# Two stacked layers of segment-recurrent attention and gated MLP: Q and K of four segments' own tokens computed ahead, kept in DRAM and read back

## The chip, the cores and the metric

The kernel runs on one core of a Trainium2 chip. The metric is the device time of one execution in microseconds (us): the median of the runs. Five engines work side by side, each on its own instructions in order: PE (TensorE; matmuls, and as PEld its weight loads), DVE (VectorE), ACT (ScalarE), POOL (GpSimd) and SP (SyncE), which issues most DMA transfers. ACT and POOL issue some as well.

## What is computed

```python
def _A_ref(x, mem0, Wq, Wk, Wv, Wo, seg_len):      # 2048 tokens of width 576, 64 segments of 32
    mem = mem0                                     # 8 memory tokens
    for s in range(n_seg):
        xs = x[:, s * seg_len:(s + 1) * seg_len, :]
        h = concatenate([mem, xs])                 # 40 rows
        q, k, v = h @ Wq, h @ Wk, h @ Wv           # 32 heads of 128
        p = softmax(where(mask, q @ k.T * scale, -1e9))
        o = einsum("hte,hed->td", p @ v, Wo)
        mem = o[:, :M]                             # the next segment's memory
        outs.append(o[:, M:])
def _B_ref(x, w1, w3, w2):                         # hidden width 4608
    return (silu(x @ w1) * (x @ w3)) @ w2
x = x + _A_ref(_layernorm(x), ...); x = x + _B_ref(_layernorm(x), ...)
x = x + _A_ref(_layernorm(x), ...); x = x + _B_ref(_layernorm(x), ...)
```

The memory makes the segments a recurrence: segment s+1 can start only when segment s has its output. The own 32 tokens of a segment in the first layer, though, depend on x alone.

## The kernel before

The work is a sequence of 72 steps. Step t handles segment t of the first layer and, from step 8 on, segment t-8 of the second (LAG = 8). Steps 0 to 7 and 64 to 71 have one layer and 40 columns; steps 8 to 63 have both, 80 columns side by side. After four segments a block of 128 tokens goes through the MLP, spread over later steps.

A step's attention works in four groups (g) of eight heads. For each of eight units (u) of four heads, qk does 32 matmuls (Q and K, four heads, four chunks of 128 of the width) and qk_tail 8 half-row matmuls for the last 64 of the width. qk_ev copies the result from PSUM to QKT, one of four buffers, in two pieces where there are two layers. Then come scores (bank<-QKT), the softmax on DVE and ACT (tiles SME, STAT, PB), the transposition of P (in one-layer steps on PE; in the others a DMA transpose issued by SP, PTS<-PB), P times V, the output projection (wo, wo_tail), and the copy of the new memory into HT. V is projected by vm, vx and vg.

All parts of the work are nodes with dependencies, buffers and modelled costs. The order of PE's nodes is written out by hand as a string of letters: FIRST for steps 0 to 15, then FOUR eleven times for four steps each, then LAST. plan places the nodes of the other engines (and of SP's DMA queue) around it by modelled times, choosing DVE or ACT for copies. Every engine then runs its list in order. The table WARM names places where em.warm issues filler matmuls (line 663), which compute nothing that is used. The weights Wq, Wk, Wv and Wo, 18.9 MB, are loaded in that order at the start by SP, with their tails and the first block of x partly by ACT; then the MLP's weights stream through two buffers each (W13, W2C).

x_in brings a block of 128 rows of x into XN; ln_stats, ln_pow, ln_norm and ln_tr normalise and transpose it, and ht_write puts it into HT, from which qk reads. The MLP's input is XTB.

Of the kernel before, what the change touches and what calls it, by code (L numbers as in the profile page):

```python
# [7 lines left out]
BF = mybir.dt.bfloat16  # L8
# [5 lines left out]
P = 128  # L14
# [16 lines left out]
WARM = {("QKt", 5): 22, ("TR", 2): 8, ("VMt", 1): 8, ("PV", 1): 5, ("TR", 3): 2, ("QK", 9): 2, ("PV", 5): 2, ("WO", 5): 3, ("TR", 7): 2, ("QK", 17): 2, ("SC", 12): 1,  # L31
        ("PV", 9): 2, ("WO", 9): 2, ("PV", 11): 1}
# [11 lines left out]
         "xr": 3, "xn": 2, "w13": 2, "w2": 2, "htt": 3}  # L44
# [14 lines left out]
class Node:  # L59
# [11 lines left out]
    def after(self, *more):  # L71
        for d in more:
# [7 lines left out]
         "WO": "O", "WOt": "o", "VX": "X", "VXt": "x", "VM": "V", "VMt": "v", "FF": "F", "FFt": "f", "VG": "G", "VGt": "g", "W2": "W", "W2b": "w"}  # L80
# [126 lines left out]
def ewh(*ns):  # L207
# [5 lines left out]
    "amQqqQQqqQSqQQqTSqSQqQTSVvxXPPTTOoPPOOooOoQqqqQQSQqQSvQqqqVTSPOQqQTTSPPXoOTOPoxOooQQqqqqQSQvVqSQQqQqqQSSTTPPOoOT"  # L213
    "TPoPOOooaVvqqQQQqqSQQSqqqQQQSTxqPTSOPXOTTooPPOOooQqqqpQQSQqVSnQvfqFqQQSfFqqQTFTSPfPTOOWoofPTFPOOooFfqqQQQSWQFqqf"
    "qQFTSqfVvqqQQQWTSSPFPFffXxWTOPoOTOPFOoooffFQqqqQWQQSFfqqVvfFQWSqQQSTFqqffQFTSPaWPOTOPFooffTFPOOooWqqQQQSqqQVSvqf"
    "FQTQWQqqqTPSQObSPoXXTTxxPOPOOoooQpQQqqqqQnSvqSFfVFfqQQQSFfqQqWSPFFPffOoOPWOFPooOofFQqqfqQWSQQQQqqqfFSFSGqfgqQQWP"
    "GSgfgFGPFOofgGPOWPOOoooFfqqQQQSfqqFWQFvSqfVQQqWSFqfqQQfPPSFOOFooPWaffOPFOooWQqqqqQQbSQQQqqSGSqgqQQPgGSOoPGggGPOO"
    "PooOoQqppQQQqqqVnnSSvfFQFfqqQQQqqfSFSwPWPOOFooffFPWPOwOooFqqffQFQWwSFfqqQQQWQqqSwSfgfGFPFQQqqGSggGPGOOPoogfFPOOo"
    "owQWQffqqFFQwQqqSWSvVqqqQQQFffSqFQPwWPSFffOOFPawooOPWOooFfqqQQWSQqqqqQQQSwbqqSQQGgSggGPGPOGogPOPOOooo"
# [23 lines left out]
def make_nodes(em, nseg, pools, o=Opt, dma_bw=230e3, load_bw=400e3):  # L243
# [125 lines left out]
    def step(t):  # L369
# [18 lines left out]
        for g in range(NG):  # L388
            qs, qe = [], []
            for u in (2 * g, 2 * g + 1):  # L390
                q = Slot("qkt", users=1)
                b = banks()
                pq = t + o.qk + o.ustep * u
                m_ = node("PE", 32 * mm80 + (0.02 if nl == 1 else 0.0), em.qk(t, u, b), deps=hx + hm[:1] + ([ld_h[u // 4]] if t == 0 else []),
                          prio=pq, mode="full", acq=[q] + b, name="QK")
                n = node("PE", 4 * mm80 + (0.014 if nl == 1 else 0.008), em.qk_tail(t, u, b), deps=hx + hm + ([ld_h[u // 4]] if t == 0 else []), prio=pq + o.qkt, mode="row",
                         acq=[q] + b, name="QKt")
                rd += [m_, n]
                me[f"QK{u}"], me[f"QKt{u}"] = m_, n
                for r in (0, 1):  # L400
                    qe.append(node("AD", ew(256, 64) if nl == 2 else ew(160), em.qk_ev(t, u, r, q, b[r]), deps=[m_, n], prio=t + o.ustep * u,
                                   rel=[b[r]], name="QKe"))
                qs.append(q)
# [73 lines left out]
    def job(j):  # L477
# [45 lines left out]
        for pp, ents, at in todo:  # L523
# [4 lines left out]
            for pr_ in (2 * pp, 2 * pp + 1):  # L528
# [8 lines left out]
                else:  # L537
# [3 lines left out]
                    ld = [node("DMA", kb(1152, 256) / dma_bw, em.load_w13(pr_, w13), prio=prio - 1, acq=[w13], lat=2.3, name="W13")]  # L541
                    lds.append(node("DMA", kb(256, 576) / dma_bw, em.load_w2(pr_, w2), prio=prio - 0.99, acq=[w2], lat=2.2, name="W2l"))
# [55 lines left out]

    x_in(0)
    ht_mem[0] = [node("DVE", 0.1, em.init_mem(0, 0), deps=[m0e], prio=-4, name="m0")]  # L600
# [27 lines left out]
class Emitter:  # L628
# [137 lines left out]
    def load_xn(self, g, xn):  # L766
        return lambda n: (self.dma if g else self.adma)(self.T.XN[:, xn.i, 0:D], self.a.x[g * P:(g + 1) * P, :])
# [70 lines left out]
    def ln_pow(self, xn):  # L838
        def f(n):
            L = self.T.LNS[:, xn.i]  # L840
            self.ch("POOL", self.nc.gpsimd.tensor_tensor(L[:, 15:16], L[:, 14:15], self.T.mhalf[:], op=ALU.pow))
        return f

    def ln_norm(self, src, xn):
        def f(n):
            L = self.T.LNS[:, xn.i]
            self.v("tensor_scalar", self.T.XN[:, xn.i, 0:D], self.src_ap(src), L[:, 12:13], L[:, 15:16],
# [124 lines left out]

    def head(self, g, j):

        return GH * g + j

    def qk(self, t, u, b):

        def f(n):
# [3 lines left out]
            for c in range(4 if first and t == 0 and u % 4 == 0 else 0):  # L983
                for _ in range(3):
                    self.mm(self.bk(b[1])[:], self.T.ident[:, 0:P], self.T.W[:, 4 + c, u * 512:(u + 1) * 512], True, True)
            for j in range(4):
                h0 = self.head(u // 2, 4 * (u % 2) + j) * E
                for kind in (0, 1):
                    for c in range(4):
                        self.mm(self.bk(b[kind])[:, j * SW:j * SW + q1 - q0], self.T.W[:, 4 * kind + c, h0:h0 + E], HTt[:, c, q0:q1],  # L990
# [3 lines left out]
    def qk_tail(self, t, u, b):  # L994
        def f(n):
            q0, q1 = self.qcols(t)
            HTt = self.ht(t)
            first = self.begin(b)
            for j in range(4):
                h0 = self.head(u // 2, 4 * (u % 2) + j) * E  # L1000
                for kind in (0, 1):
                    rr = slice(kind * R64, (kind + 1) * R64)
                    self.mm(self.bk(b[kind])[:, j * SW:j * SW + q1 - q0], self.T.W[rr, 8, h0:h0 + E], HTt[rr, 4, q0:q1],
# [313 lines left out]
def kernel(  # L1317
# [42 lines left out]
    T.mhalf = sp.tile([P, 1], F32, name="mhalf")  # L1360
# [6 lines left out]
    T.LNS = sp.tile([P, pools["xn"], 16], F32, name="LNS")  # L1367
    T.QKT = sp.tile([P, pools["qkt"], 2, 4, 2 * QW], BF, name="QKT")
# [11 lines left out]
    T.HTT = sp.tile([P, pools["htt"], 2, 2 * P], BF, name="HTT")  # L1380
    T.M0 = T.XTB[:].rearrange("p a b -> p (a b)")[:, 0:D]
# [3 lines left out]
    nc.gpsimd.memset(T.mhalf[:], -0.5)  # L1385
# [60 lines left out]
```

## Time and profile before

| | us |
|---|---|
| median of 3 runs (lowest to highest) | 2618.39 (2617.04 to 2626.04) |
| the profiled execution, its own time | 2624.02 |
| its span in the trace | 2622.2 |
| PE busy | 2567.1 |
| DVE busy | 2009.5 |
| ACT busy | 1266.8 |
| mean granted clock of PE | 0.999 |

The span is the time between the first and the last event of the trace. A busy PE counts filler matmuls as well as work, and the ends of matmuls are modelled, since they are pipelined: the spacing of many in a row says what one costs, not the duration of a single one. An idle time is put down to what ended last before the instruction could go; "issue" is a wait for nothing that the profile shows.

### The profile page before, as it was taken

The page shows a single profiled execution, that of the slowest core. Times are in us where ns is not written, and L with a number is a line of the kernel's source. Part 1 is how long each engine was busy: PE and PEld are TensorE (multiplying, and loading weights), DVE is VectorE, ACT ScalarE, POOL GpSimd, SP SyncE. Part 2 cuts the span into 40 slices and gives each one's busy share as a digit, 9 for nine tenths or more (in the row PEclk, how much of TensorE's full clock was granted, in tenths as well). Part 3 has the DMA queues.
Part 4 walks back from the last instruction along what each step waited for, and adds up shares of the span by engine and source line. Part 5 has one row for each costly group of instructions (what it writes and reads, how often), then busy time and mean ns, then how long its engine had stood idle before and what let it go on. Part 6 is the DMA issues. An engine that isn't in the chain of part 4 may idle for free.

```text
span 2622.2 us, 131462 instructions
## 1 busy us (share of the span) xinstructions
PE 2567.1 (98%) x58447; PEld 2205.6 (84%) x58498; DVE 2009.5 (77%) x5145; ACT 1266.8 (48%) x3743; POOL 196.1 (7%) x253
## 2 busy tenths in 40 slices
PE   6999999999999999999999999999999999999998
PEld 4788888888888888888888888888888888888887
DVE  4778777787787688777867877786787778777877
ACT  2655453544545354454535445453544545445553
POOL 1100000000001000000000000010000000010000
PEclk9999999999999999999999999999999999999999
DMA  9064746565464656555465655546465554554447
GB/s 326 4 181 126 193 103 154 126 152 136 126 139 115 148 128 153 135 126 141 115 148 128 155 133 127 144 109 151 128 156 132 126 143 112 128 146 129 123 131 258
DMA packets 680217, 369.58 MB, mean 141 GB/s; under 512 B 233592, under 2 KB 669824, under 8 KB 679008
## 3 DMA queue, kind: packets, MB, share of 16 engines
q1 hardware_dynamic: 675968, 353.23, 52.5%
q8 instruction: 457, 7.49, 1.2%
q0 software_dynamic: 3024, 6.93, 0.9%
q10 hardware_dynamic: 656, 1.02, 0.2%
q14 instruction: 112, 0.92, 0.1%
HBM read 304.95 MB, written 2.36 MB: 117 GB/s over the span
## 4 chain that ended last, share of the span: by engine, by line
PE 90%; DMA 4%; DVE 3%; SPq 1%; issue 1%; ACT 1%; ACTq 0%; DVEq 0%
PE bank L653 90%; DMA PTS<-PB 2%; DMA W<-in_B_w_dram 1%; SPq L672 1%; DVE STAT L669 1%; DVE PB L669 1%; DVE SME L669 1%; DMA WV<-in_A_Wv_dram 0%; DVE HTT L669 0%; DMA W<-in_A_Wk_dram 0%; ACT V L666 0%; DVE V L669 0%; PE bank L663 0%; DMA W2C<-in_B_w_dram 0%; ACT HT L666 0%
## 5 line engine op out<-in xcount | busy, mean ns | idle before, releaser
L653 PEld LDWEIGHTS <-W 128*128 128x128 bf16 (+2 forms) x32096 | 1252.3, 100 | 121.3 <-issue 66.1
L653 PE MATMUL bank<-HT,W 128*128 128x80 bf16 (+3 forms) x23040 | 792.9, 197 | 9.6 <-ACT HT L666 5.4
L653 PE MATMUL bank<-XTB,W 128*64 128x256 bf16 (+5 forms) x9056 | 662.5, 264 | 4.5 <-DMA W<-in_B_w_dram 4.2
L666 ACT ACTIVATE QKT<-bank 128x192 bf16<-128x192 f32 (+4 forms) x1674 | 382.2, 312 | 274.5 <-PE bank L653 268.7
L653 PE MATMUL bank<-OT,WO 128*128 128x80 bf16 (+3 forms) x11520 | 411.1, 198 | 1.3 <-issue 1.3
L653 PEld LDWEIGHTS <-WO 128*128 128x128 bf16 (+1 forms) x11520 | 380.4, 102 | 27.6 <-issue 13.4
L666 ACT ACTIVATE V<-bank 64x512 bf16<-64x512 f32 (+1 forms) x589 | 333.0, 585 | 136.7 <-PE bank L653 129.8
L653 PE MATMUL bank<-WV,HT 128*32 128x512 bf16 (+4 forms) x3430 | 355.9, 381 | 6.8 <-issue 4.3
L653 PE MATMUL bank<-W2C,HTT 128*64 128x288 bf16 (+1 forms) x3152 | 322.1, 287 | 0.7 <-DMA W2C<-in_B_w_dram 0.6
L666 ACT ACTIVATE HTT<-bank 128x512 bf16<-128x512 f32 (+1 forms) x324 | 173.1, 550 | 284.0 <-PE bank L653 283.1
L669 DVE SCALAR_TENSOR_TENSOR XR<-bank,XR 128x288 f32<-128x288 f32 x574 | 243.4, 448 | 59.0 <-PE bank L653 53.4
L669 DVE TENSOR_REDUCE STAT<-SME 104x8 f32<-104x320 f32 (+1 forms) x576 | 273.8, 475 | 12.2 <-ACT SME L666 5.0
L669 DVE TENSOR_TENSOR PB<-SME,STAT 40x128 bf16<-40x128 f32 (+4 forms) x912 | 275.1, 336 | 8.1 <-issue 0.2
L653 PEld LDWEIGHTS <-HT 128*32 128x32 bf16 (+4 forms) x3472 | 147.5, 98 | 140.3 <-issue 24.9
L1092 POOL MEMSET PB<- 128x1024 bf16 x142 | 134.8, 951 | 1742.7 <-DMA PTS<-PB 1219.4
L653 PEld LDWEIGHTS <-HTT 128*64 128x64 bf16 (+1 forms) x3232 | 231.4, 105 | 35.7 <-issue 5.6
L669 DVE SCALAR_TENSOR_TENSOR HTT<-HTT,bank 128x512 bf16<-128x512 bf16 (+1 forms) x324 | 200.9, 620 | 69.7 <-ACT HTT L666 65.8
L666 ACT ACTIVATE OT<-bank 128x320 bf16<-128x320 f32 (+1 forms) x389 | 145.1, 402 | 203.8 <-PE bank L653 196.6
L669 DVE TENSOR_TENSOR HTT<-HTT,bank 128x512 bf16<-128x512 bf16 (+1 forms) x324 | 203.5, 628 | 28.0 <-DVE HTT L669 0.9
L666 ACT ACTIVATE SME<-SME 104x320 f32<-104x320 f32 (+1 forms) x288 | 135.0, 469 | 180.9 <-DVE SME L669 179.0
L669 DVE CAST V<-bank 64x512 bf16<-64x512 f32 (+1 forms) x275 | 188.3, 685 | 40.8 <-PE bank L653 36.4
L669 DVE TENSOR_TENSOR SME<-bank,maskb 104x320 f32<-104x320 f32 (+1 forms) x288 | 138.9, 483 | 39.4 <-PE bank L653 36.1
(61 smaller groups left out, 1400.8 us busy)
## 6 DMA issues: line engine op xcount, KB each, us to landing
W<-in_B_w_dram SPq DMA_DIRECT2D x604, 256.0 KB, 3.5
W2C<-in_B_w_dram SPq DMA_DIRECT2D x302, 288.0 KB, 3.5
W<-in_B_w_dram SPq DMA_DIRECT2D x604, 32.0 KB, 3.5
W<-in_B_w_dram SPq DMA_DIRECT2D x8, 1024.0 KB, 13.0
W<-in_A_Wq_dram SPq DMA_DIRECT2D x9, 512.0 KB, 9.9
WO<-in_A_Wo_dram SPq DMA_DIRECT2D x4, 1152.0 KB, 16.8
XR<-in_A_x_dram POOLq DMA_DIRECT2D x16, 288.0 KB, 2.9
WV<-in_B_w_dram SPq DMA_DIRECT2D x4, 1152.0 KB, 12.3
```

Of the source, the lines that this page charges most:

```text
L653: self.ch("PE", self.nc.tensor.matmul(out, lhsT=lhsT, rhs=rhs, start=start, stop=stop, skip_group_check=True, **k))
L666: self.ch("ACT", self.nc.scalar.activation(*a, **k))
L669: self.ch("DVE", getattr(self.nc.vector, fn_)(*a, **k))
L672: self.ch("SP", self.nc.sync.dma_start(out=out, in_=in_))
L1092: return lambda n: self.ch("POOL", self.nc.gpsimd.memset(self.pbt(pb), 0.0))
```

## The change

A new function hold, called after the first block of x, loads two more blocks of x (rows 256 to 511, segments 8 to 15) on ACT's DMA queue, normalises and transposes them, and copies the even segments 8, 10, 12 and 14 into XTB. Eight units (KP with 32 matmuls, KPt with 8) multiply these 128 columns with Wq and Wk, two copies bring each unit's result from PSUM into a W2C buffer (KPe), and SP stores it to a DRAM tile SX (KPs). In steps 8, 10, 12 and 14 (PRE) the matmuls of qk and qk_tail take 48 columns where they took 80: the second layer's 40 and the first layer's 8 memory columns, read as two pieces of 24. A load by SP (KPl) brings the unit's 64 KB into QX, one buffer, and a copy (KPc) puts it into QKT; qk_ev copies three pieces. The MLP's weight loads come after the last store. The constant of ln_pow moves into the tile LNS. FIRST and WARM are written anew; FOUR and LAST are as they were.

```diff
-WARM = {("QKt", 5): 22, ("TR", 2): 8, ("VMt", 1): 8, ("PV", 1): 5, ("TR", 3): 2, ("QK", 9): 2, ("PV", 5): 2, ("WO", 5): 3, ("TR", 7): 2, ("QK", 17): 2, ("SC", 12): 1,
-        ("PV", 9): 2, ("WO", 9): 2, ("PV", 11): 1}
+WARM = {("QKt", 1): 30, ("Ktr", 2): 10, ("KPt", 1): 1, ("SC", 4): 1, ("VXt", 1): 6, ("PV", 1): 2, ("WO", 1): 1}
+PRE = (8, 10, 12, 14)
...
-    "amQqqQQqqQSqQQqTSqSQqQTSVvxXPPTTOoPPOOooOoQqqqQQSQqQSvQqqqVTSPOQqQTTSPPXoOTOPoxOooQQqqqqQSQvVqSQQqQqqQSSTTPPOoOT"
+    "amcqcqkQQKkqSqQQqKqSQQqkTQSQqTSxXVvKPTOPoTPOPOooOoQqqqQQSQqqqVvQqSQQQSTqXqxPSTKPOTOPooTOPokOoaQqqqQSVvqqqQQSQQqq"
...
+                if held:
+                    x = Slot("qx")
+                    ld = node("DMA", kb(P, 256) / load_bw, em.held_load(t, u, x), deps=[held_st[u]], prio=pq - 0.5, acq=[x], lat=2.2, name="KPl")
+                    qe.append(node("AD", (0.05 + 256 / 1200, 0.065 + 256 / 1920), em.held_copy(u, q, x), deps=[ld, m_], prio=pq, rel=[x], name="KPc"))
...
-                    ld = [node("DMA", kb(1152, 256) / dma_bw, em.load_w13(pr_, w13), prio=prio - 1, acq=[w13], lat=2.3, name="W13")]
+                    ld = [node("DMA", kb(1152, 256) / dma_bw, em.load_w13(pr_, w13), deps=held_st[-1:], prio=prio - 1, acq=[w13], lat=2.3, name="W13")]
...
+    def hold():
+        wr = []
+        for i in (0, 1):
+            xn = Slot("xn")
+            ld = node("ACT", 0.6, em.load_xn(PRE[2 * i] // 4, xn, True), prio=-70 + i, acq=[xn], name="ldxn", lat=9.0)
+            wr += ln_nodes("K", xn, xn, [ld], -3 + i, [(em.held_write(i), ewh(320), [m0t])])
+        mm = (P / 2.4 + 2.5) / 1000
+        for u in range(8):
+            b = banks()
+            prio = 0.5 + 0.1 * u
+            m_ = node("PE", 32 * mm, em.held_qk(u, b, False), deps=wr + [ld_h[u // 4]], prio=prio, mode="full", acq=b, name="KP")
+            n = node("PE", 4 * mm + 0.008, em.held_qk(u, b, True), deps=wr + [ld_h[u // 4]], prio=prio, mode="row", acq=b, name="KPt")
+            w = Slot("w2")
+            es = [node("AD", ew(512), em.held_ev(r, w, b[r]), deps=[m_, n], prio=prio, acq=[w], rel=[b[r]], name="KPe") for r in (0, 1)]
+            held_st.append(node("DMA", kb(P, 1024) / load_bw, em.held_store(u, w), deps=es, prio=prio, rel=[w], lat=2.2, name="KPs"))
+            last_up.extend([m_, n])
...
+    def held_cols(self, v):
+        return bass.AP(v.tensor, v.offset, [list(x) for x in v.ap][:-1] + [[QW + 16, 2], [1, 24]])
...
+            elif self.held(t):
+                self.cp(n, dst[:, :, 64:SW], src[:, :, 0:16])
+                self.cp(n, dst[:, :, 0:MEM], src[:, :, 16:24])
+                self.cp(n, dst[:, :, QW:64], src[:, :, 24:48])
```

In the letters c is a new transposition, K and k the new units' matmuls and tails.

On VectorE, the first instructions after the clearing of the banks. Before:

```order
L669 BN_STATS LNS<-XN 128x6 x2
L669 BN_AGGR LNS<-LNS 128x2
L669 TENSOR_SCALAR LNS<-LNS 128x1
L669 TENSOR_SCALAR XN<-XN,LNS 128x576
L669 COPY XN<-XN 128x64
```

And in the changed kernel:

```order
11 L696 BN_STATS LNS<-XN 128x6 x2
12 L696 BN_AGGR LNS<-LNS 128x2
13 L696 TENSOR_SCALAR LNS<-LNS 128x1
14 L696 BN_STATS LNS<-XN 128x6 x2
15 L696 BN_AGGR LNS<-LNS 128x2
16 L696 TENSOR_SCALAR LNS<-LNS 128x1
17 L696 TENSOR_SCALAR XN<-XN,LNS 128x576
18 L696 COPY XN<-XN 128x64
```

The statistics of the second block (rows 14 to 16) now stand ahead of the normalisation of the first (rows 17 and 18), which PE's first transposition reads.

On SP, the issues after the four loads of Wo. Before (W_84 is the tile W13, the MLP's up weights, W2C its down weights):

```order
8 L672 DMA WO<-in_A_Wo_dram 128x8x576 x4
9 L672 DMA W_84<-in_B_w_dram 128x4x256 x2
10 L672 DMA W_84<-in_B_w_dram 64x256 x2
11 L672 DMA W2C<-in_B_w_dram 128x2x576
12 L672 DMA W_84<-in_B_w_dram 128x4x256 x2
```

And now (SX is the DRAM tile, QX the buffer of the loads back):

```order
8 L699 DMA WO<-in_A_Wo_dram 128x8x576 x4
9 L699 DMA SX<-W2C 128x4x256 x2
10 L699 DMA QX<-SX 128x256
11 L699 DMA SX<-W2C 128x4x256
12 L699 DMA XN<-in_A_x_dram 128x576
13 L699 DMA SX<-W2C 128x4x256 x5
14 L699 DMA W_83<-in_B_w_dram 128x4x256 x2
```

The eight stores and the first load back stand where the first weights of the MLP stood; these follow the last store.

On SP in step 10, about the DMA transposes of P (PTS<-PB). Before:

```order
104 L1095 DMA_TRANSPOSE PTS<-PB 128x8x112 x2
105 L672 DMA W2C<-in_B_w_dram 128x2x576 x2
106 L672 DMA W_84<-in_B_w_dram 128x4x256 x2
107 L672 DMA W_84<-in_B_w_dram 64x256 x2
108 L1095 DMA_TRANSPOSE PTS<-PB 128x8x112
109 L672 DMA W_84<-in_B_w_dram 128x4x256 x2
```

And in the changed kernel:

```order
110 L699 DMA QX<-SX 128x256
111 L699 DMA W_83<-in_B_w_dram 128x4x256 x2
112 L699 DMA W_83<-in_B_w_dram 64x256 x2
113 L699 DMA QX<-SX 128x256
114 L699 DMA W2C<-in_B_w_dram 128x2x576 x2
115 L699 DMA QX<-SX 128x256
116 L699 DMA W_83<-in_B_w_dram 128x4x256 x2
117 L699 DMA W_83<-in_B_w_dram 64x256 x2
118 L1180 DMA_TRANSPOSE PTS<-PB 128x8x112
```

The loads back stand between the weight loads and the transposes, one by one.

More of the change, by code (lines that the diff above doesn't have):

```diff
@@ L764, in load_o, with load_xn @@
         return lambda n: self.dma(self.T.WO[:, g * GH:(g + 1) * GH, :], self.a.wo[g * GH:(g + 1) * GH].rearrange("h e d -> e h d"))
[L766 to L767 removed]
+    def load_xn(self, g, xn, early=False):
+        return lambda n: (self.dma if g and not early else self.adma)(self.T.XN[:, xn.i, 0:D], self.a.x[g * P:(g + 1) * P, :])
     def load_x(self, g, xr):
```

85 lines of the change are left out of this document (67 added, 18 removed).

## The prediction

> **What bounds the kernel now.** I read the page first: busy shares, the slices, the chain that ended last.
>
> ```profile
> PE 2567.1 (98%) x58447; PEld 2205.6 (84%) x58498; DVE 2009.5 (77%) x5145; ACT 1266.8 (48%) x3743; POOL 196.1 (7%) x253
> PE   6999999999999999999999999999999999999998
> DMA  9064746565464656555465655546465554554447
> PE 90%; DMA 4%; DVE 3%; SPq 1%; issue 1%; ACT 1%; ACTq 0%; DVEq 0%
> ```
>
> TensorE carries the time, except in the first slice, where it is 60% busy and the DMA engines are full. Whatever saves matmul time saves time, if nothing else then ends last. Next, the busy time in stretches; columns are the stretch, then its length, busy time of PE, PEld, DVE, ACT, POOL, the granted clock, DMA share, GB/s. The cuts at 59, 82, 103 and 124 us are the ends of steps 0 to 3; 234, 367 and 520 us are those of steps 7, 11 and 15.
>
> ```profile
> 0.00:23.60 23.60, 5.11 (x22) 2.19 (x23) 9.03 (x20) 2.24 (x5) 5.69 (x17) 1.00 0.93 299
> 23.60:43.80 20.20, 18.71 (x408) 13.05 (x408) 11.23 (x31) 4.90 (x15) 0.00 (x0) 1.00 1.02 410
> 43.80:59.00 15.20, 12.29 (x311) 8.42 (x313) 7.79 (x15) 6.92 (x16) 2.51 (x3) 1.00 1.09 363
> 59.00:82.00 23.00, 21.90 (x662) 17.46 (x665) 16.38 (x47) 13.11 (x37) 2.43 (x3) 1.00 0.08 25
> 82.00:103.00 21.00, 20.01 (x647) 16.89 (x644) 15.82 (x45) 12.53 (x37) 1.84 (x2) 1.00 0.02 4
> 103.00:124.00 21.00, 20.56 (x682) 16.87 (x677) 16.98 (x45) 14.10 (x41) 1.84 (x2) 1.00 0.02 5
> 234.00:367.00 133.00, 128.31 (x3190) 110.42 (x3193) 102.33 (x282) 66.56 (x209) 9.78 (x12) 1.00 0.66 154
> 367.00:520.00 153.00, 152.12 (x3150) 128.93 (x3150) 119.25 (x308) 72.43 (x211) 11.06 (x14) 1.00 0.56 135
> ```
>
> TensorE is idle for 18.5, 1.5 and 2.9 us in the three stretches of step 0, then for 1.1, 1.0 and 0.4 us in steps 1 to 3. A busy PE isn't all work: line 663 issues filler matmuls in waits. Its groups in 23.6 to 59 us and in 59 to 124 us:
>
> ```profile
> L663 PE MATMUL bank<-W,ident 128*128 128x512 bf16 x42 | 9.9, 379 | 0.7 <-ACT V L666 0.3 <-issue 0.3
> L663 PE MATMUL bank<-W,ident 128*128 128x512 bf16 x11 | 3.5, 377 | 0.5 <-issue 0.5
> ```
>
> So step 0 holds about 14 us of waiting after the first projections (1.5 + 2.9 + 9.9), and steps 1 to 3 hold 2.5 idle and 3.5 filled, 6.0 us. That is the room in which new work is free. From step 16 on the order of every engine is the same in both kernels, so the whole difference arises in the first 521 us. I make the sum against the profiled execution, 2624.0 us (span 2622.2), which lies 5.6 us above the median of the runs, 2618.4; differences carry over.
>
> **Term 1, the projections in steps 8, 10, 12, 14.** Eight units a step, each of 32 matmuls and 8 half-row tails, go from 80 columns to 48. The traces show 80 columns (first two rows, 234 to 520 us) and 40 (last two, 59 to 124 us):
>
> ```profile
> L653 PE MATMUL bank<-HT,W 128*128 128x80 bf16 x2048 | 79.5, 202 | 0.7 <-ACT HT L666 0.7
> L653 PE MATMUL bank<-HT,W 64*128 64x80 bf16 x512 | 15.1, 199 | 0.0
> L653 PE MATMUL bank<-HT,W 128*128 128x40 bf16 x768 | 22.0, 179 | 0.4 <-issue 0.4
> L653 PE MATMUL bank<-HT,W 64*128 64x40 bf16 x192 | 4.4, 178 | 0.0
> ```
>
> 79.5/2048 is 38.8 ns and 22.0/768 is 28.6; the tails take 29.5 and 22.9. At the price of 40 columns, 4 x 256 x 10.2 ns = 10.4 us and 4 x 64 x 6.6 ns = 1.7 us go, 12.1 in all. On the straight line between 40 and 80, 48 columns give 4/5 of that, 9.7. 48 is near 40 and the price of 40 may be a floor, so I take **-11** (ends -9.7 and -12.1). The trace can't tell the ends apart. [...]
>
> **Term 2, the units computed ahead.** Eight units of 32 matmuls of 128 columns and 8 tails. The nearest row is a run of 16 up-projections of that shape:
>
> ```profile
> 313.46 1.06 PE L653 MATMUL bank<-XTB,W 128*128 128x128 bf16 x16
> ```
>
> Taking off 0.22 us for the last one's own passage, 15 starts in 0.84 us are 56 ns, so a unit is 1.8 us and about 0.3 for tails: 2.1 us. The order puts three units in step 0, one in step 1, two in step 2, two in step 3. The five in steps 1 to 3 cost 10.5 us, against 6.0 us of room. If all the room is used, +4.5; if none (the waits are for softmax chains that stay as long), +10.5. Each unit also adds two copies out of PSUM, half of them on VectorE, which is 71 to 81% busy there. The filler has gone from these steps, which speaks for the lower end. I take **+5**.
>
> The three units of step 0 lie beside the weights' arrival. PE's start (start us, length; the last row is the first use of V's weights):
>
> ```profile
> 17.59 3.59 PE L653 MATMUL bank<-W,ident 128*128 128x512 bf16 x9 [4.13 <-DMA W<-in_A_Wk_dram]
> 23.66 4.16 PE L653 MATMUL bank<-HT,W 128*128 128x40 bf16 x160
> 28.28 4.70 PE L663 MATMUL bank<-W,ident 128*128 128x512 bf16 x21 [0.16 <-issue]
> 43.79 0.63 PE L653 MATMUL bank<-WV,HT 64*32 64x512 bf16 x16
> ```
>
> In the new order 40 fillers and the second new transposition stand ahead of the first projection. VectorE now takes statistics of a second block of x before it normalises the first, so PE starts at about 17 us. Some seven fillers then run at 0.40 us (3.59/9, early) and 33 at 0.224 (4.70/21): about 28 us with the transpositions, where projections began at 23.7. That delay is covered: before, 21 fillers followed at 28.3 while the second half of Wq and Wk came. From 28.5, all step 0 projections, scores and two new units need some 15 us and end near 43.8, when V's weights have come; the third unit stands in the copying of V. What stays is the two added blocks of x, 2 x 144 KB at 410 GB/s ahead of the weights: **+0.7** (from -1 to +3; if the cover failed, up to 5).
>
> **Term 3, the way back through DRAM.** Eight stores of 256 KB follow Wo on SP's queue, and the first MLP weights wait behind the last one (end of step 3). Their first use is in step 4, behind that step's first projections, and they land in 3.5 us (first row below): I cost that at nothing; if the cover fails, 3 us once. In the four steps SP issues 32 loads of 64 KB into one buffer. Load u+1 waits until copy u has emptied it, and SP is in order: behind a load that waits stand weight loads and the transposes of P. So loads form a loop of issue, landing, copy. The rows nearest to such a load, with the median us from issue to landing last:
>
> ```profile
> W<-in_B_w_dram SPq DMA_DIRECT2D x604, 256.0 KB, 3.5
> PTS<-PB SPq DMA_TRANSPOSE x224, 3.0
> XN<-in_A_x_dram SPq DMA_DIRECT2D x15, 144.0 KB, 3.7
> out_dram<-XN SPq DMA_DIRECT2D x1, 72.0 KB, 1.6
> L666 ACT ACTIVATE QKT<-bank x192: 218/330/472, 239.0 to 506.4; 128x192 bf16<-128x192 f32 x50, 128x128 bf16<-128x128 f32 x50, 128x256 bf16<-128x256 f32 x46, 128x64 bf16<-128x64 f32 x46
> ```
>
> With 0.3 us for the copy the loop is between 1.9 and 4.0 us; I take 3.3, by the transposes. What the order leaves: counting the matmuls ahead of the last scores in each of the four steps at the spacing of their weight loads in the trace gives 21 to 24 us. The same count over steps 8 to 15 of before gives 261 us where the stretches show 286, so 23 to 26 us in fact; less 1.8 for the first copy, seven loops have about 3.1 us each. At 3.3, 0.2 x 7 x 4 = 5.6 us: **+6** (0 if the loop is 3.1 or less, 25 at 4.0). SP's issues can stretch it. A transposed P shows what it is to stand behind weights:
>
> ```profile
> 258.25 3.25 SPq L672 DMA_DIRECT2D W<-in_B_w_dram  x4
> 261.60 1.26 SPq L1095 DMA_TRANSPOSE PTS<-PB  x1
> 266.92 0.45 PE L653 MATMUL bank<-PTS,V 128*128 128x80 bf16 x8 [1.18 <-DMA PTS<-PB]
> ```
>
> Issued 3.35 us after the weights, used 5.3 us after that, with 1.2 us of idle PE. [...]
>
> The copies grow too: three pieces for two, and the copy from DRAM's buffer, 24 more instructions a step of about 0.25 us, on two engines. ACT is half idle in these stretches and VectorE 77%, so I count them in the loop alone; with no cover, 1 us a step, inside the range.
>
> **Sum.** 2624.0 - 11 + 5 + 0.7 + 6 = 2624.7, that is +0.7, and on the median 2618.4 + 0.7 = **2619 us**. Its own range, by the terms' nearer ends, is 2612 to 2626.
>
> **Rivals.**
> - *The loop decides.* One buffer, seven loops ahead of the last scores, SP in order. It costs from 3.1 us a loop on; at 4.0 (the row of x, 3.7, and the copy) it costs 25 us instead of 6: 2638. For it: the rows from the same queue, and the 5.3 us behind weights. Against: 64 KB is less than either row, and in part of the loops the scores wait for something else anyway. Chance 0.20.
> - *All hides.* The loop stays under 3.1 us, steps 1 to 3 use all their room (+4.5), and three waits of the old order are not met again: -11 + 4.5 + 0.7 - 5.1 = -10.9, 2607 to 2608. The waits are in the next rows: an issue wait of 1.5 us that ends at 152.7, after which the granted clock is 0.50 for 3 us (1.5 of work lost), and the waits for P in 234 to 521 us (2.1). Against: their cause, bursts of weights, remains. Chance 0.17.
>
> ```profile
> 152.71 0.94 PE L653 MATMUL bank<-HT,W 128*128 128x40 bf16 x31 [1.48 <-issue]
> 154.00:157.00 3.00, 3.00 (x42) 2.29 (x43) 2.66 (x6) 0.47 (x1) 0.00 (x0) 0.50 0.11 12
> PE bank L653 <- DMA PTS<-PB: 2.1, 2, 1.2
> ```
>
> - *The units hide nowhere.* Steps 1 to 3 keep their waits: +10.5 for +5, 2624 to 2625. For it: VectorE's share in these steps. Against: 3.5 us of filler that was there only to pass time. Chance 0.12.
> - *It doesn't do what it says.* 48 columns read in two pieces of 24 cost what 80 did: no -11, 2630. Against: 40 columns show 10 ns less. Chance 0.06.
>
> The forecast has 0.45. **Range 2605 to 2640**: it takes in most of the first two rivals. A measurement of this kernel can tell about 0.5%, 13 us, from no change: faster by more (under 2605.3) 0.10, from the second rival's better half; slower by more (over 2631.5) 0.22, the first rival and a little of the last; within, 0.68.
>
> **What would show it.** The group of 48-column projections at 28.6 to 31 ns; step 0 ending at 59 to 61 us with the first projection near 28; steps 1 to 3 taking 69 to 71 us where they took 65; in steps 8, 10, 12, 14 waits of scores on copies whose releaser is the DMA from DRAM, some 1.5 us a step. No such waits would prove the loop short, and the time would be nearer 2612; SP waiting for most of those steps and transposes landing late would be the first rival. Steps 0 to 3 shorter than before would overturn term 2.

## The result and the profile after

| | before | changed |
|---|---|---|
| median of the runs, us (lowest to highest) | 2618.81 (2617.04 to 2626.04) | 2646.74 (2638.46 to 2648.59) |
| ratio of changed to before, 95% interval | | 1.0095 (1.0066 to 1.0124) |
| profiled execution, us | 2624.02 | 2645.09 |
| its span, us | 2622.2 | 2643.3 |

The change costs 0.95%. The prediction was 2619, with a range to 2640. In the profiled pair the difference is 21.1 us; the medians differ by 27.9, because before's profiled execution was 5.2 us above the median in this table and the changed kernel's 1.7 us below. The ledger below is that of the profiled pair.

The page of the changed kernel, its engines and the shares of the chain that ended last:

```profile
PE 2578.4 (98%) x58813; PEld 2212.8 (84%) x58856; DVE 2018.2 (76%) x5176; ACT 1275.5 (48%) x3838; POOL 198.2 (8%) x255
PE 87%; DMA 7%; DVE 4%; issue 1%; SPq 1%; ACT 1%; ACTq 0%; DVEq 0%
```

PE still carries the time, but its share of the chain fell from 90 to 87% and that of DMA rose from 4 to 7%: the loss is waiting for transfers. Step ends, read from the last output projection of each step in both traces to about 0.2 us, say where. The changed kernel is later by 5.1 us at the end of step 0, 8.4 at the end of step 3, 4.1 at step 7, 14.6 at step 15, 19.0 at step 71 and 21.1 at the end of the span.

The stretches of the changed kernel; columns as in the prediction. The first row runs from its first projection to the first use of V's weights; the next three are steps 1, 2 and 3, the last two steps 8 to 11 and 12 to 15:

```profile
28.30:50.90 22.60, 18.12 (x441) 15.02 (x439) 11.76 (x31) 6.29 (x19) 0.00 (x0) 0.85 1.04 403
...
64.00:86.40 22.40, 22.08 (x708) 18.64 (x704) 17.95 (x52) 14.38 (x38) 2.46 (x3) 1.00 0.07 20
86.40:108.30 21.90, 21.90 (x722) 19.77 (x722) 16.21 (x48) 12.73 (x36) 1.90 (x2) 1.00 0.15 40
108.30:132.30 24.00, 23.68 (x740) 20.40 (x736) 18.14 (x48) 14.73 (x38) 1.90 (x2) 1.00 0.10 27
...
238.60:381.00 142.40, 130.90 (x3275) 109.81 (x3272) 105.17 (x294) 72.29 (x258) 9.80 (x12) 0.99 0.69 152
381.00:535.20 154.20, 149.17 (x3131) 123.79 (x3132) 120.10 (x309) 76.27 (x258) 11.49 (x14) 1.00 0.59 140
```

Steps 1 to 3 are nearly without idle PE now (0.6 us, where before had 2.5): they end up 3.3 us longer and hold five units. New in the first row is a granted clock of 0.85 (third from the end). And in the last two rows, steps 8 to 15, PE is busy for 280.1 of 296.6 us. Before, in the same steps:

```profile
234.40:520.60 286.20, 280.63 (x6342) 239.45 (x6345) 221.54 (x589) 139.00 (x420) 20.84 (x26) 1.00 0.61 144
```

The same busy time, and 10.4 us more in the stretch: all of it is idle PE, 16.5 us where there were 5.6. This is the largest part of the loss. What ended the idle time of steps 8 to 15 in the changed kernel (total us, times, longest):

```profile
PE bank L680 <- DMA PTS<-PB: 6.6, 5, 2.3
PE bank L680 <- ACT QKT L693: 4.2, 5, 2.0
PE bank L680 <- DMA W2C<-in_B_w_dram: 1.9, 1, 1.9
PE bank L680 <- ACT HT L693: 1.4, 3, 0.8
PE bank L680 <- DMA W<-in_B_w_dram: 1.2, 3, 0.7
```

The second row is the loop of loads that the prediction spoke of. The first is larger: transposes of P that come late, 6.6 us where before showed 2.1.

**The saving is there.** The projections of steps 8, 10, 12 and 14:

```profile
L680 PE MATMUL bank<-HT,W 128*128 128x48 bf16 x1024 | 30.1, 183 | 1.1 <-ACT HT L693 1.1
L680 PE MATMUL bank<-HT,W 64*128 64x48 bf16 x256 | 7.2, 182 | 0.0
```

30.1/1024 is 29.4 ns and 7.2/256 is 28.1; with 38.8 and 29.5 before, 9.6 + 0.4 = 10 us are gone.

**The start.** PE's order of time in step 0 (start us, length; rows of the trace that matter):

```profile
16.10 8.60 PE L690 MATMUL bank<-W,ident 128*128 128x512 bf16 x30
...
28.31 1.77 PE L680 MATMUL bank<-HT,W 128*128 128x40 bf16 x64
...
34.16 1.70 PE L680 MATMUL bank<-HT,W 128*128 128x40 bf16 x62 [1.01 <-issue]
...
40.35 1.88 PE L680 MATMUL bank<-HT,W 128*128 128x40 bf16 x54 [1.54 <-issue]
...
46.55 0.71 PE L680 MATMUL bank<-HT,W 128*128 128x40 bf16 x22 [1.59 <-issue]
...
50.92 4.32 PE L680 MATMUL bank<-WV,HT 64*32 64x512 bf16 x80
```

The first projection comes at 28.3 us, as forecast, in part by luck: PE began at 14.7 us, not at 17, and the fillers and transpositions took that much longer. V's weights are used at 50.9, not 43.8: between them lie three waits of PE for nothing that the profile shows, 4.1 us in all, each 128 matmuls after the one before it (the rows between hold 62 + 66 and 54 + 74). The DMA engines are full in that time (share 1.04). Behind the second and the third the granted clock halves; behind the second, in stretches of 2 us:

```profile
40.00:42.00 2.00, 1.65 (x51) 1.60 (x52) 0.11 (x1) 0.84 (x3) 0.00 (x0) 0.64 0.99 400
42.00:44.00 2.00, 2.00 (x56) 1.79 (x56) 1.58 (x6) 0.44 (x1) 0.00 (x0) 0.51 1.06 384
```

Two spells of 3.4 us each at a granted clock of 0.50 (from 40.55 and from 47.38 us) lose 3.4 us of work. 4.1 + 3.4 is about the 7.1 us by which V comes later. Before had one such wait, of 0.9 us, among the 238 matmuls between its first second-half weights at 28.3 us and V; the changed kernel passes 441 there. 2 us are won back before step 0 ends.

The page lists a queue by the name of instruction (transfers, MB, share):

```profile
q8 instruction: 460, 7.54, 1.2%
```

These are 460 transfers of 16.4 KB, and the page counts 117669 matmuls and weight loads on PE, 256 for each transfer, that is 128 matmuls with their weight loads. In the trace such transfers start at 31.8, 38.0 and 44.1 us, and each of the three waits ends 2.4 to 2.5 us after one. That PE waits there for its own next instructions is the author's inference from these times; no run varied it, so it is not shown.

**The late transposes.** Steps 8 and 10 on SP's queue, beside the matmuls that wait. Step 8:

```profile
250.55 3.18 SPq L699 DMA_DIRECT2D W<-in_B_w_dram  x4
254.04 0.34 SPq L699 DMA_DIRECT2D QX<-SX  x1
254.49 1.35 SPq L1180 DMA_TRANSPOSE PTS<-PB  x1
255.93 3.19 SPq L699 DMA_DIRECT2D W<-in_B_w_dram  x4
259.24 0.52 SPq L699 DMA_DIRECT2D QX<-SX  x1
259.59 0.48 PE L680 MATMUL bank<-PTS,V 128*64 128x80 bf16 x16 [1.93 <-DMA PTS<-PB]
...
262.82 0.42 ACT L693 ACTIVATE QKT<-QX 128x256 bf16<-128x256 bf16 x1 [1.39 <-DMA QX<-SX]
263.26 0.34 SPq L699 DMA_DIRECT2D QX<-SX  x1
...
266.31 0.42 ACT L693 ACTIVATE QKT<-QX 128x256 bf16<-128x256 bf16 x1 [2.03 <-DMA QX<-SX]
...
266.77 0.37 PE L680 MATMUL bank<-QKT 128*64 128x40 bf16 x13 [1.97 <-ACT QKT L693]
```

Issuing four weight loads keeps SP for 3.2 us. The transpose behind them goes out at 254.5 and its result is used 5.1 us later, with 1.9 us of idle PE. The load behind the next four is issued at 259.2 and its copy starts at 262.8, 3.6 us later; the next load follows at 263.3 and its copy 3.1 us behind it; then come scores, 2.0 us late. A loop is 4.0 and 3.5 us here, where 3.3 was forecast.

Step 10, where the idle time also costs clock:

```profile
326.06 2.14 SPq L699 DMA_DIRECT2D W<-in_B_w_dram  x4
328.29 2.03 SPq L1180 DMA_TRANSPOSE PTS<-PB  x1
...
332.75 0.46 PE L680 MATMUL bank<-PTS,V 128*128 128x80 bf16 x8 [2.34 <-DMA PTS<-PB]
...
334.00:337.00 3.00, 3.00 (x47) 2.83 (x44) 2.44 (x6) 0.31 (x2) 0.00 (x0) 0.52 1.02 136
```

The first part of P was written by 324.4 us; its transpose stands behind weights, PE waits 2.3 us, and from 334.1 the clock is halved for 3.4 us.

### The profile page after: what moved, and what is told of

The parts are those of the page before. It is cut to its first block, busy times and chain, and to the rows that moved or that the text cites. A ratio compares the mean times of both kernels' runs of the same rounds, so it can differ in the third digit from the quotient of the medians.

```text
span 2643.3 us, 132432 instructions
## 1 busy us (share of the span) xinstructions
PE 2578.4 (98%) x58813; PEld 2212.8 (84%) x58856; DVE 2018.2 (76%) x5176; ACT 1275.5 (48%) x3838; POOL 198.2 (8%) x255
## 4 chain that ended last, share of the span: by engine, by line
PE 87%; DMA 7%; DVE 4%; issue 1%; SPq 1%; ACT 1%; ACTq 0%; DVEq 0%
PE bank L680 86%; DMA PTS<-PB 3%; DMA W<-in_B_w_dram 2%; SPq L699 1%; DVE PB L696 1%; DVE STAT L696 1%; DVE HTT L696 1%; DMA W2C<-in_B_w_dram 1%; PE bank L690 1%; DMA QX<-SX 0%; DVE SME L696 0%; DMA XN<-in_A_x_dram 0%; DVE V L696 0%; DVE XR L696 0%; ACT HT L693 0%
## 5 line engine op out<-in xcount | busy, mean ns | idle before, releaser
L680 PE MATMUL bank<-HT,W 128*128 128x80 bf16 (+4 forms) x23040 | 785.0, 196 | 13.5 <-ACT HT L693 6.8
L680 PE MATMUL bank<-XTB,W 128*64 128x256 bf16 (+5 forms) x9360 | 684.2, 262 | 7.5 <-DMA W<-in_B_w_dram 7.3
L693 ACT ACTIVATE QKT<-bank 128x64 bf16<-128x64 f32 (+4 forms) x1745 | 383.4, 304 | 242.3 <-PE bank L680 232.6
L696 DVE TENSOR_TENSOR HTT<-HTT,bank 128x512 bf16<-128x512 bf16 (+1 forms) x324 | 203.4, 628 | 27.9 <-DVE HTT L696 0.5
```

The lines of the kernel that those rows point to most:

```text
L680: self.ch("PE", self.nc.tensor.matmul(out, lhsT=lhsT, rhs=rhs, start=start, stop=stop, skip_group_check=True, **k))
L693: self.ch("ACT", self.nc.scalar.activation(*a, **k))
L696: self.ch("DVE", getattr(self.nc.vector, fn_)(*a, **k))
```

## The experiments

Two theories were left for steps 8 to 15. *The loop*: the loads took back the saving and more, the prediction's term 3 at a larger size. *The order* (theory O from the fifth kernel on): the new order costs by itself, loads or no loads. Letters in an expectation are explained there. Times are compared by the ratio to before, measured beside each group of kernels, since before's own median moved between 2619 and 2626; "steps 8 to 15" is the time from the end of step 7 to the end of step 15 in the profile.

### Taking the change apart

```diff
# e3_units_unused
     def held(self, t):
-        return t in PRE
+        return False
```

> The eight units are computed and stored, but steps 8, 10, 12, 14 compute all 80 columns and load nothing back. Theory A, the way back costs about 12 us in these steps and the 48 columns save 11: the two nearly cancel, 2643 to 2648. Theory C, the way back costs little and the loss comes from the units and the new order ahead of step 8: the saving alone is lost, 2655 to 2658.

Measured: 2645.34, ratio 1.0086 (1.0068 to 1.0104), the time of the changed kernel: without the loads and without the saving, nothing changes, as the loop's theory had it too. Steps 8 to 15 take 298.4 us:

```profile
237.70:536.10 298.40, 290.13 (x6408) 244.05 (x6403) 230.94 (x607) 138.62 (x416) 20.87 (x26) 0.99 0.59 138
```

```diff
# e4_loaded_once
+                    if (t, u) == (PRE[0], 0):
                     x = Slot("qx")
                     ld = node("DMA", ..., em.held_load(t, u, x), ...)
+                        once.extend([x, ld])
+                    x, ld = once
```

> Leaves out 31 of the 32 loads: one block is loaded once and all 32 copies read it (the second to last units' values are not the right ones). No load waits for a buffer, and SyncE's queue is free of them. Theory A: all that the way back costs goes, 12 to 13 us, 2632 to 2634, and steps 8 and 10 are 4 to 7 us shorter each than in the changed kernel. Theory C: unchanged, 2643 to 2647.

Measured: 2635.70, ratio 1.0054 (1.0036 to 1.0072). Steps 8 to 15, and the largest of PE's waits there:

```profile
236.50:525.00 288.50, 277.66 (x6412) 231.75 (x6404) 225.21 (x603) 148.12 (x516) 21.33 (x26) 1.00 0.64 143
PE bank L683 <- DMA PTS<-PB: 6.3, 7, 2.6
```

The PE order is that of the changed kernel in both, so the pairs price two terms: 48 columns for 80 without loads save 298.4 - 288.5 = 9.9 us, and 31 loads cost 296.6 - 288.5 = 8.1. Each figure is from one profile (before's two differ by 2.4 us in these steps, see Scatter). The 8.1 are read from the waits nearly whole: 4.2 of scores on copies, 1.9 of one wait for W2C, 1.7 of half clock. The transposes are as late without the loads, 6.3 us for 6.6. But before took 286.2. With 80 columns and no loads the new order takes 12.2 us more: a term that the prediction did not have.

```diff
# e8_no_units (on e4): no blocks of x ahead, no units, no stores
     x_in(0)
-    hold()
# FIRST without the letters c, K and k; the one load reads x
```

> Leaves out the two blocks of x, the eight units, their copies and stores, and all loads but one; the 48 columns stay (the copies bring in a block of x, not Q and K). Against the run with one load it prices the units and stores. By the prediction's term 2 that is 5 to 6 us; by the traces, where steps 0 to 7 end 4.1 us later than before, about 4 to 9, the larger if work moved out of these steps hides a part. Expected 2624 to 2629. If the whole loss were in the way back, it would be the same as the run with one load.

Measured: 2641.53, ratio 1.0074 (1.0057 to 1.0091). The forecast of 2624 to 2629 was missed: without the units the kernel is slower than e4. Steps 1 to 3 took 72.0 us, more than the 68.3 with the units: the time of the units turned into waits, and waits into half clock (0.82 and 0.86 between 75 and 128 us). Steps 8 to 15 took 290.9, again with late transposes (7.0 us). Yet up to there e8 is ahead: its step 15 ends at 523.5 us, e4's at 525.1. It falls behind in steps 16 to 71, where it takes 8 us more than e4 in the same order (see Scatter). So the times don't price the blocks and units; by the end of step 15 e4, which has them, is 1.6 us behind.

```diff
# e13_order_alone (on e8): 80 columns, no load
     def held(self, t):
-        return t in PRE
+        return False
```

> The work of before in the new order: no blocks of x ahead, no units, no stores, no loads, 80 columns in all steps; 30 fillers ahead of the first tails are kept, ten others are left out with the transposition that carried them. Theory O (the order alone costs): by the end of step 15 it is 6 to 13 us later than before, 2625 to 2632 us in all. Rival (the order alone costs nothing): within 3 us of before, 2616 to 2622.

Measured: 2646.19, ratio 1.0089 (1.0067 to 1.0110): above the range of 2625 to 2632, and as much as the whole change. That the two are equal is chance: of 24.8 us over before in the profiles, 7.3 lie in steps 1 to 3, where the units' places stand empty and half clock takes 11.9 us of work, and 8.6 in steps 16 to 71. Steps 8 to 15:

```profile
235.80:536.20 300.40, 289.98 (x6412) 244.34 (x6406) 230.81 (x607) 138.83 (x416) 20.94 (x26) 0.99 0.63 138
PE bank L682 <- DMA PTS<-PB: 6.2, 5, 3.4
```

14.2 us more than before, with no load in the queue, and the same 6 us of waits for transposes. So the loop alone can't be the cause, and theory O stands as far as this goes. It isn't the order alone, though: e3 and e13 keep the changed kernel's tiles, and no run has the old letters, 80 columns and these tiles together.

### Why the order is as it is

```diff
# e10_old_steps: FIRST's letters of steps 4 to 15 as before
```

> All of the change is kept; only the order written out for steps 4 to 15 is put back to the order of before (steps 0 to 3 keep the new order with the units). Theory O (the new order of steps 4 to 15 itself costs the 6 us or so that the loads and the start don't explain): step 15 ends about 6 us earlier than in the changed kernel, about 2641 us. Rival B (bursts of weights and the loads cost that in any order): the time stays within 3 us of the changed kernel, 2646. Rival L (the old order leaves the loop of loads less room than the new one): slower than the changed kernel, 2650 or more, with more waits of scores on copies.

Measured: 2687.36, ratio 1.0245 (1.0219 to 1.0271); steps 8 to 15 take 330.8 us.

```profile
PE bank L680 <- ACT QKT L693: 36.6, 14, 4.5
```

Rival L. The old order leaves the loop no room: scores wait for loaded halves 14 times, up to 4.5 us, and half clock takes another 22 us of work (granted clock 0.93 in these steps). The new order saves 34 us of this, at the price of the 12 of e3.

```diff
# e16_old_loaded_once: old orders, and e4's single load
```

> Both old orders (step 0 and steps 4 to 15 as before, units added), 48 columns in four steps, but only the first of the 32 loads: the loop is taken away and the order that was bent to make room for it too. Theory O (the new order of steps 8 to 15 costs 10 to 14 us, whatever the loads do): the saving shows, step 15 ends 3 to 8 us earlier than before, about 2612 to 2616. Rival (48 columns leave the same waits in any order, since chains other than PE set the scores): step 15 ends 3 us or more later than before, 2622 or more.

Measured: 2651.02, ratio 1.0104 (1.0089 to 1.0119); steps 8 to 15 take 298.4. The rival held: not even with the loop gone does the old order give the saving. Waits for transposes are 9.0 us there, and half clock takes 10.2 us of work (granted clock 0.97). In step 14 one matmul waits 3.6 us for a copy into V, and another for a transpose:

```profile
500.79 0.69 PE L683 MATMUL bank<-PTS,V 128*128 128x80 bf16 x8 [3.14 <-DMA PTS<-PB]
```

So O can't mean "the new letters are worse": with 48 columns and one load they take 10 us less than the old ones (288.5 for 298.4). One reading is that an order hides its waits at one set of durations and not at another, and that what counts is how transposes and weights fall against each other on SP. Another is that the new tiles make transfers slower in any order (see Scatter). These runs don't tell the two apart.

### What stands in SP's queue

```diff
# e14_no_weights (on the changed kernel), e15_before_no_weights (on before)
-   em.load_w13(pr_, w13)
+   (lambda n: None) if 8 <= s0 < 16 else em.load_w13(pr_, w13)
-   em.load_w2(pr_, w2)
+   (lambda n: None) if 8 <= s0 < 16 else em.load_w2(pr_, w2)
```

> The changed kernel without the loads of MLP weights in steps 8 to 15 (the MLP of these steps multiplies by weights that lie in the buffers already); every other instruction, in the same order. In the changed kernel steps 8 to 15 take 11 us longer than before, with 11 us more idle PE. Theory Q (that idle time comes from SP's queue, where transposes of P and loads of Q and K stand behind weights): steps 8 to 15 fall from 298 us to 287 or less, the time to 2633 to 2636, and with before treated alike (the next kernel) the new one is the faster by 0 to 6 us in these steps. Rival R (the order itself: softmax chains and the loop of loads set the waits): steps 8 to 15 fall by no more than they do in before treated alike, 1 to 4 us, and the difference stays at 8 to 11 us.

> The kernel before without the loads of MLP weights in steps 8 to 15, the partner of the kernel ahead. Its PE waits in these steps for transposes and weights are 2.8 us in the profile, so it gains 2 to 5 us by either theory: 2614 to 2617. A larger gain would mean that matmuls themselves run slower beside the weights' transfers.

> The changed kernel with only the first of the 32 loads and without the MLP weight loads of steps 8 to 15: the fourth corner of a square of weights and loads. Steps 8 to 15 took 296.6 us with both, 288.5 with weights alone, 282.6 with loads alone; before without the weights took 282.5. If the saving is there once nothing stands in SP's queue: the matmul work is 10 us less and 3.6 us of MLP work moved in, so 276 to 277 us, and the time 2624 to 2626. If the loads cost the same 8 us with and without weights: 274 to 275. If the order itself holds waits that neither causes: 280 or more.

Measured: e14 2630.80, ratio 1.0028 (1.0016 to 1.0039); e15 2620.35, ratio 0.9983 (0.9973 to 0.9992); e18 (both edits, e14's and e4's) 2633.06, ratio 1.0028 (1.0013 to 1.0043). e14 came out as theory Q had it (287 us or less), e18 as its last case (280 or more). Steps 8 to 15 of e14, and PE's waits there:

```profile
238.50:521.00 282.50, 276.82 (x6408) 231.89 (x6401) 224.66 (x603) 148.29 (x516) 21.26 (x26) 1.00 0.24 46
PE bank L680 <- DMA PTS<-PB: 1.5, 2, 0.9
PE bank L680 <- ACT QKT L693: 1.4, 4, 0.7
```

| steps 8 to 15, us | with MLP weights | without |
|---|---|---|
| changed | 296.6 | 282.5 |
| changed, one load | 288.5 | 280.6 |
| before | 286.2 | 282.5 |

Weights cost 14.1 us beside the loads, 7.9 without them, and 3.7 in before; loads cost 8.1 us beside the weights and 1.9 alone. Single profiles of before differ by 2.4 us, so the 14.1, 8.1 and 7.9 are clear and the 3.7 and 1.9 hardly. Without weights the changed kernel and before take the same time in these steps. So the gap of 10.4 us is the weights meeting the new order (7.9 - 3.7 = 4.2) and the loads (6.2 more). Leaving the weights out takes issues off SP's queue and traffic off the DMA engines at once (their share falls from 0.63 to 0.24 in the changed kernel), so which of the two acts isn't shown. A load's landing, in the changed kernel and then without the weights:

```profile
QX<-SX SPq DMA_DIRECT2D x31, 64.0 KB, 2.6
```

```profile
QX<-SX SPq DMA_DIRECT2D x31, 64.0 KB, 1.9
```

Even e18 doesn't show the whole saving: 280.6 against 282.5. By an estimate, the count of matmuls at the spacing of their shapes in the traces, the new order does 5.6 us less work in steps 8 to 15: the saving of 10.4 less 4.8 of other work that was moved in, mostly from steps 4 to 7. Of these 5.6, 1.9 are seen; e18's idle PE of 5.2 us, against 2.1 in e15, takes most of the rest (copies to HT and OT).

```diff
# e20_transposes_first: a transpose of steps 8 to 16 passes the one or two weight loads right ahead of it in SP's order
+            for m in moved:
+                seq.remove(m)
+            i = seq.index(n)
+            seq[i + 1:i + 1] = moved
```

> The changed kernel, with one thing moved in SP's order in steps 8 to 16: a transpose of P that stood right behind one or two weight loads now stands ahead of them (where no matmul in between reads them), so these weights wait until P is ready. Theory Q (transposes behind weights are the largest part of the waits): PE's waits for transposes in steps 8 to 15 fall from 6.6 us to 2 or less and the time by 3 to 6 us, to 2641 to 2644. Rival (what the transposes win the weights lose, the queue being too full): the waits for weights rise from 3.1 us by as much, and the time stays at 2646 or rises.

> The old order of step 0 (which ended 4 us earlier than the new one, with units in place of fillers) together with transposes ahead of weights. If the two gains add up: 3 to 4 us under the kernel that has only the transposes moved, about 2637 to 2640. If the gain of the start is lost again in later waits, as it was by the end of step 15 when it was tried alone: the same as that kernel within 2 us.

Measured: e20 2684.14, ratio 1.0230 (1.0210 to 1.0250); e21 (with e11's start) 2682.42, ratio 1.0226 (1.0205 to 1.0247). PE's waits in e20 from 238.6 to 560 us:

```profile
PE bank L700 <- DMA W<-in_B_w_dram: 14.6, 8, 5.5
PE bank L700 <- DMA W2C<-in_B_w_dram: 6.0, 5, 1.9
PE bank L700 <- DMA PTS<-PB: 4.8, 4, 2.2
```

The rival, and far beyond its size: weights held until P is ready cost 20.6 us where they had cost 3.1, and the transposes gained only 1.8. e21 is its second case, within 2 us of e20. This one rule for the queue only moves the loss, and adds to it.

```diff
# e2_pool_queue: GpSimd issues the loads
-   ld = node("DMA", kb(P, 256) / load_bw, em.held_load(t, u, x), ...
+   ld = node("SWD", 1.0, em.held_load(t, u, x), ...
# e17_act_queue: ScalarE issues them
+   ld = node("ACT", 0.5, em.held_load(t, u, x), ...
```

> The 32 loads from DRAM are issued by GpSimd's queue instead of SyncE's; nothing else is edited (the planner orders SyncE's issues anew). Theory A1, SyncE's order is what costs in steps 8 to 14 (a load that waits for the buffer, or stands behind weight issues, and transposes of P behind it): 8 to 13 us of the 26 go, 2632 to 2638. Theory A2, the loop through one buffer costs by its own length: at most 3 us go, 2642 or more. Rival, the costs lie before step 8: no change, 2645.

> The loads of Q and K are issued by ScalarE, on its own queue, in place of SyncE. Theory Q: they no longer stand behind weights, and transposes no longer behind loads; waits of scores on copies fall from 4.2 us to 2 or less, and the time to 2636 to 2642. Rival (a load that waits for its buffer holds up the engine that issues it, as it did on GpSimd's queue, where the time rose to 2669): ScalarE's other work comes late, waits for its copies rise, 2650 or more.

Measured: e2 2668.87, ratio 1.0178 (1.0157 to 1.0198); e17 2657.58, ratio 1.0126 (1.0107 to 1.0145). In e17 PE waits 11.2 us for copied halves in steps 8 to 15, where the changed kernel had 4.2. e17's rival held; e2 came out 24 us above the 2645 of its rival, and only "2642 or more" covers it. Either second queue makes it worse. Landing takes 2.8 us from ScalarE and 2.9 from GpSimd, not less than the 2.6 from SP. The plan also placed the other nodes anew, so these two runs don't price the queue alone.

### The start

```diff
# e11_old_start: before's letters in step 0, with units for fillers
+   "amQqqQQqqQSccKkKkqQQqTSqSQqQTSVvxXKkPPTTOoPPOOooOo..."
+WARM = {("TR", 2): 8, ("VMt", 1): 8, ("PV", 1): 1}
# e12_old_both: e11 and e10 together
```

> All of the change is kept; only step 0 goes back to the order of before, with two units in place of the 22 fillers ahead of the second half of the weights and one unit ahead of PV. Theory S (the 5 us at the start come from fillers and projections that run while the DMA engines are full, behind a late first projection): step 0 ends within 2 us of its end in before (59 to 61 us), and the time is 3 to 5 us under the changed kernel, about 2642. Rival W (the two added blocks of x and the arrival of V's weights set the end of step 0 in any order): step 0 ends near 64 us again and the time stays at 2646.

> Both orders put back: step 0 of before with three units in it, steps 4 to 15 of before; steps 1 to 3 keep the new order with five units. Theories O and S together: about 2636 to 2638, what is left over 2619 being the loop of loads and the five units less the saving. If neither holds: 2646. If only S holds: 2642.

Measured: e11 2643.31, ratio 1.0078 (1.0060 to 1.0096); e12 2689.50, ratio 1.0261 (1.0234 to 1.0288). In e11:

```profile
23.02 4.16 PE L680 MATMUL bank<-HT,W 128*128 128x40 bf16 x160
...
28.62 4.64 PE L680 MATMUL bank<-XTB,W 128*128 128x128 bf16 x80 [0.47 <-DVE XTB L696]
...
36.24 0.38 PE L680 MATMUL bank<-HT,W 128*128 128x40 bf16 x9 [1.09 <-issue]
...
44.82 0.62 PE L680 MATMUL bank<-WV,HT 64*32 64x512 bf16 x16
```

Projections start at 23.0 although the two blocks of x come first here too; two units stand where 22 fillers stood; V's weights are used at 44.8, and step 0 ends at 60.0, 1.1 us after before's. So theory S: 4 of the 5.1 us at the start were the order's, and the extra blocks can cost no more than the 1.1 left, near the 0.7 forecast. By the end of step 15, though, e11 is 14.3 us behind before, where the changed kernel is 14.6 behind: it loses the gain again in steps 1 to 15. The ratio is 0.0017 lower than the changed kernel's, less than the intervals can tell. e12 fits none of its cases: with the old letters its steps 8 to 15 take 337.8 us, much as in e10.

### Scatter

> The kernel before, profiled a second time. In the changed kernel steps 16 to 71, where every engine's order is that of before, took 4.5 us longer. Theory N (scatter between executions): the second profile of before shows these steps 2 us or more longer than the first. Rival (something of the change goes on acting): they agree within 1 us.

Measured: 2621.55 us, one execution. Steps 8 to 15 took 283.8 us here, 2.4 less than in the first profile, so the gap of 10.4 is 10 to 13. Steps 16 to 71 took 2058.0 us, against 2056.4 in the first profile: between the two cases.

More runs say more. In steps 16 to 71 every engine's order is the same in all kernels, and so are the bytes moved. In the three profiles of before's tiles (before, e9, e15) these steps take 2056.4 to 2059.7 us, and the DMA engines are busy for a share of 0.54. In all fifteen profiles with the changed kernel's tiles they take 2060.9 (the changed kernel) to 2073.7 us (e3 2067.8, e8 2069.6, e13 2065.0), and the share is 0.56 or 0.57. On the changed kernel's page the MLP's weights land in 4.0 us, where the line in the prediction has 3.5:

```profile
W<-in_B_w_dram SPq DMA_DIRECT2D x604, 256.0 KB, 4.0
```

So something of the change goes on acting and makes transfers slower. It is neither the units nor the loads nor the letters of step 0 or of steps 4 to 15, since each of these is taken back in some of the fifteen. Left is what all fifteen share, such as the new tiles (QX, SX and the constant in LNS), much of the order of steps 1 to 3, and the buffers' numbers after it; no run separates these. At most 17 us in 56 steps would be some 2.5 us in eight, less than the 12.2 of e3, if it acts alike in steps 8 to 15; that isn't known.

## Why the prediction was wrong

- **Term 1, -11: right.** 10 us by the rows, 9.9 by e3 and e4.
- **Term 2, +5: right in kind.** Steps 1 to 3 took 68.3 us, 3.3 more, under the lower end (4.5): idle and filler were used up, and a little more. "The units hide nowhere" fell. In e8, which leaves the room empty, these steps took 72.0 us, with 10.2 us of work lost to half clock.
- **The start, +0.7: wrong, +5.1.** The step that failed: "From 28.5, all step 0 projections, scores and two new units need some 15 us and end near 43.8". Their work was counted at the dense spacing. Under full DMA engines (share 1.04), PE waited three times, 1.0 to 1.6 us, 128 matmuls apart, and twice the granted clock fell to 0.50 for 3.4 us, and V's weights were used at 50.9 us. e11, with step 0 in the old order, ends it 4 us earlier. The prediction's "if the cover failed, up to 5" had the size.
- **Term 3, +6: right in kind, too small.** 8.1 us by e4. Waits of scores on copies were 4.2 us (1.1 a step, 1.5 forecast); the rest is mostly one late W2C (1.9) and half clock (1.7), neither of which the term held. The loop ran at 3.5 to 4.0 us in step 8, not 3.3. The transposes behind weights, which the prediction showed beside the loop, are as late without loads.
- **The missing term, the largest failed step.** The sum held the edits and left the rewritten order of steps 4 to 15 at nothing; in "what the order leaves" it read that order only for the loop's room. e3 shows 12.2 us in steps 8 to 15 with neither loads nor 48 columns: 4.8 of moved work, most of it given back by steps 4 to 7 (4.3 us shorter in the changed kernel), 1.7 by half clock, 2.7 of idle PE, and some 3 that stay unresolved within busy time. Whether the letters do this or the slower transfers that come with the new tiles is open.
- **"The whole difference arises in the first 521 us": wrong, +6.6.** The order is the same from step 16 on, as the prediction says, but not the time: 4.5 us more in steps 16 to 71, with slower transfers, and 2.1 after step 71, where half clock takes 2.3 us more than in before (granted clock 0.91, against 0.96).

The ledger of the profiled pair: start +5.1, units +3.3, steps 4 to 7 -4.3, steps 8 to 15 +10.4 (order +12.2, saving -9.9, loads +8.1), after step 15 +6.6: 21.1. Of the rivals, "the loop decides" was nearest in time, for part of the reason.

Open stay the 3 us within busy time, whether the waits called "issue" are waits for instructions, and what makes the transfers slower in steps 16 to 71 and how much of the 12.2 it is. None of the kernels with the changed kernel's tiles beat before.

## What to carry to other kernels

A saved matmul counts only if what releases the next one comes earlier too: here 10 us of PE work went, and waits for transposes, loads and weights, with the half clock behind them, took more. When an order is rewritten, cost the new order with the old work as a term of its own, and look at each short transfer that now stands behind a long issue. Here an idle place in a stretch where the DMA engines were full (share 1.04) was no free room for many small matmuls: among 441 of them lay three waits, 4.1 us. And compare the stretches that the edit doesn't touch: here they weren't the same either.

## What the runs showed of the hardware

PE's granted clock fell to 0.50 for 3.4 us behind waits of 1.54 and 1.59 us in step 0 and of 2.34 us in step 10, and in before behind the wait of 1.48 us that the prediction shows. Waits of 1.93 and 1.97 us in step 8 had no half clock behind them (granted clock 1.00 from 255 to 275 us), so here the length of one wait alone didn't decide it.

From 28.3 to 50.9 us, with a DMA share of 1.04, PE waited 1.01, 1.54 and 1.59 us, the second and the third time 128 matmuls behind the wait before; in steps 1 to 3, with a share of 0.07 to 0.15, it was idle for 0.6 us in 68.3. Each of the three waits ends 2.4 to 2.5 us after the start of a transfer on the queue named instruction, and the page has one such transfer to 256 matmuls and weight loads of PE, that is 128 matmuls with their weight loads. What PE waited for isn't shown by this.
